# Batch 0 of a Fourier-and-mixer kernel without its feature fold: all 256 features in two products, with the carried weights and the first token layer interleaved anew

## The chip, the cores and the metric

The kernel runs on one core of one Trainium2 chip. Times are device microseconds (us) of that core, median of several executions; lower is better. Executions of one kernel differ (the six of before spread over 1.35 us or 0.22%), so a change of one microsecond needs many runs and a look at where in the execution it arises.

The engines are PE (matrix products), PEld (its weight loads), DVE, ACT and POOL (elementwise work) and SP (issues transfers). "L519" in a line of the profile is line 519 of that kernel's source. Line numbers differ between the two kernels, but tile names do not.

## The reference

```python
# x: (8, 3008, 256), w_tok1: (3008, 256), w_tok2: (256, 3008),
# w_ch1: (256, 1536), w_ch2: (1536, 256); output float32
def attn(x):
    X = np.fft.fft(x, axis=1)        # over the 3008 tokens
    X = np.fft.fft(X, axis=2)        # over the 256 features
    return X.real.astype(np.float32)

def mixer(x, w_tok1, w_tok2, w_ch1, w_ch2):
    xt = x.transpose(0, 2, 1)
    h = np.maximum(xt @ w_tok1, 0.0) @ w_tok2      # token layers
    u = x + h.transpose(0, 2, 1)
    h2 = np.maximum(u @ w_ch1, 0.0) @ w_ch2        # channel layers
    return u + h2
```

The kernel factors the long Fourier transform (3008 = 64 x 47). It adds each row of x to its mirror row (`xp` + `xm`), takes a first stage of 47 points (`pz`, copied to `z`), a second stage over the features (`pw`, copied to `w`), and a third stage (`py`, `pq`) that yields the transform. The first token layer is not applied to the transform. Its weights are carried through the third stage instead (`hp`, `hq`: the token weights `w1p`, `w1m` times the turned tables of that stage), so that it can start on `w`. Then come the second token layer (`pu`) and the channel layers, whose first product has the name `pc`.

## The kernel before

Only the opening, batch 0 ahead of its first channel product `pc`, is touched. These are its parts in the kernel before.

```python
# Turning a table: 2 x 6 transposes on PE and two wide copies on ACT,
# then a product with the mirrored identity, copied on ACT with a sign.
def turn(tab, tts, warm):
    for h in range(2):
        pt = psum.tile([P, 1024], FP16, tag="mm", name="pt", bufs=3)
        for g in range(6):
            nc.tensor.transpose(out=pt[:, g * P:(g + 1) * P],
                                in_=tab[:, 6 * h + g, :], identity=ident[:])
        copy(0, tts[0][:, 768 * h:768 * h + 768], pt[:, 0:768])
    filler(warm)                    # 128-column products that keep PE busy
# ... turn_rows(tts, sgn, warm): three products "pr", three ACT copies ...

# One group of carried weights: four products and one 512-wide copy.
def carried(tts, dst, g2, e):
    ph = ps_mm("ph")
    for k in range(2):
        g = 2 * g2 + k
        o = ph[:, k * DTOK:(k + 1) * DTOK]
        nc.tensor.matmul(o, lhsT=tts[0][:, g * P:g * P + P], rhs=w1p[:, g, :],
                         start=True, stop=False)
        nc.tensor.matmul(o, lhsT=tts[1][:, g * P:g * P + P],
                         rhs=w1m[:, NG - 1 - g, :], start=False, stop=True)
    copy(e, dst[:, 2 * g2:2 * g2 + 2, :].rearrange("p g k -> p (g k)"), ph[:])

def fold(b, engs):
    # ... for each of four slices of the tokens:
    tt(out=xp[:, t, 1:D], in0=xp[:, t, 1:D], in1=xm[0:KR, rv, D - 1:0:-1], op=add)
    # the feature fold, even and odd parts (removed for batch 0):
    tt(out=eo[:, t, 1:129], in0=xp[:, t, 1:129], in1=xp[:, t, 255:127:-1], op=add)
    tt(out=eo[:, t, 129:256], in0=xp[:, t, 1:128], in1=xp[:, t, 255:128:-1], op=sub)

def front(b):
    # ... first stage: 8 groups of products pz from eo, each copied into z ...
    for g in range(NG):                                   # NG = 12
        pw = ps_f("pw")
        nc.tensor.matmul(pw[:, 131:WD], lhsT=zb, rhs=td1[:], start=True, stop=True)
        nc.tensor.matmul(pw[:, 0:131], lhsT=za, rhs=td0[:], start=True, stop=True)
        copy(0, w[:, g, 132:WD], pw[:, 132:WD])                    # ACT
        nc.vector.scalar_tensor_tensor(                            # DVE
            out=w[:, g, 0:131], in0=alt[:], scalar=pw[:, 131:132],
            in1=pw[:, 0:131], op0=AT.mult, op1=AT.add)
        yield
    # ... batch 0: the mirror product (needs every w), tok1(0), third(0), tok1(1),
    #     each token half ending in a relu on ACT, then pu, then pc ...
```

The order in which the pieces of the opening are issued, engine by engine, is this schedule. The tables `tp` and `tq` are finished before it starts.

```python
turn(tp, tts_p, 8)
turn_rows(tts_p, 1.0, 0)
pieces = fold(0, [nc.vector] * 4)
take(pieces, 6)
table_d()
take(pieces, 6)
own = front(0)
take(own, 2)
turn(tq, tts_q, 4)
take(own, 4)
turn_rows(tts_q, -1.0, 0)
take(own, 2)
filler(8)
take(own, 2)
for g2 in range(2):
    carried(tts_p, hp, g2, g2)
for g2 in range(NG // 2):
    if g2 < 5:
        take(own, 2)
    if g2 < 4:
        carried(tts_p, hp, g2 + 2, 0)
    carried(tts_q, hq, g2, g2 < 4)
take(own, 5)
filler(12)
```

## Time and profile before

The kernel had a median of 610.72 us in three runs (609.71 to 610.97). The profiled execution took 609.52 us.

| event in the profile of before | us |
|---|---|
| first add on x (DVE) | 12.25 |
| first product `pw` | 23.29 |
| mirror product (all of `w` is copied) | 30.39 |
| products `pu` (second token layer) go on, after one at 33.59 and a wait for a relu | 35.15 |
| first product `pc` (channel layer) | 36.62 |

From the page of before: the span, busy time by engine, the granted PE clock in 40 slices of 15 us, and the last chain by engine.

```profile
span 607.7 us, 15619 instructions
PE 586.5 (97%) x6278; PEld 420.0 (69%) x6278; DVE 453.8 (75%) x1018; ACT 442.7 (73%) x996; POOL 150.1 (25%) x233
...
PEclk9999999999999999999999999999999999999999
...
PE 91%; DVE 4%; ACT 4%; issue 1%; DVEq 0%
```

PE is busy for 97% of the span and holds 91% of the chain. What the change can win lies ahead of the first `pc`, and there the chain is another one. This is the chain of before up to that point, as start, duration and what ran.

```profile
12.27 0.84 ACT tq L240
13.13 0.84 ACT tq L240
13.99 1.52 ACT tt L284 x2
...
17.79 0.96 ACT z L284 x2
18.75 1.38 ACT tt L284 x2
...
22.21 1.03 DVE z L282 x2
23.29 0.23 PE pw L460
...
25.29 0.53 DVE w L463 x2
25.82 0.60 DVE hq L282
...
34.68 0.43 ACT uu L501
35.15 0.96 PE pu L552 x3
...
36.78 1.42 PE pc L592 x6
```

The opening ran on ACT until about 20 us (sines of the tables, and the wide copies of the turned tables), then on DVE, whose `w` and `hq` lines alternate in rounds of 1.13 us. PE holds only about 2.2 us of this chain before 30 us. From the timeline of before (start, busy time, engine, line, operation, output and inputs, shapes, and in brackets how long the engine had been idle and what ended it):

```profile
12.25 0.23 DVE L411 TENSOR_TENSOR xp<-xp,xm 94x16 f16<-94x16 f16 x1
...
36.62 1.58 PE L592 MATMUL pc<-ut,wc1p 128*128 128x512 f16 x6
```

One reading needs a warning. The row PEclk shows full speed from the first slice, and a table by stretches does so too, as in this line of before (stretch in us, its length, PE busy time and instructions, granted clock, share of the transfer engines, GB/s).

```profile
17.22:20.63 3.41, 3.05 (x33) 1.00 1.40 218
```

Here the clock column says 1.00. Yet the starts of neighbouring 128-column products are 107 ns apart in that stretch, against 55 to 57 ns later. The trace has no clock record ahead of the first switch, at 20.63 us, and the column counts time without a record as full speed. So before's PE ran at half rate until 20.63 us.

### The profile page before, as it was taken

Reading aid. Unit: us, or ns where it says so; the run is one execution under the profiler, and the core shown is the slowest. Engines: PE = TensorE matmul, PEld = TensorE weight load, DVE = VectorE, ACT = ScalarE, POOL = GpSimd, SP = SyncE. Lnnn points to the kernel's source line nnn. Section 1 sums busy time; section 2 is a strip of 40 time slices with the busy share of each in tenths; the row PEclk is TensorE's granted clock in tenths of the full one; section 3 lists DMA queues with packets and bytes.
Section 4 is the critical chain, followed back from the end, with each engine's and each line's share of the span. In section 5 each row is a group of like instructions: output and inputs, shape, how many; then the busy total and the mean of one; then the engine's idle time right before and its main releaser. Section 6 shows DMA issues by size and latency. Waiting matters only on the chain.

```text
span 607.7 us, 15619 instructions
## 1 busy us (share of the span) xinstructions
PE 586.5 (97%) x6278; PEld 420.0 (69%) x6278; DVE 453.8 (75%) x1018; ACT 442.7 (73%) x996; POOL 150.1 (25%) x233
## 2 busy tenths in 40 slices
PE   1999999999999999999999999999999999999996
PEld 1756767667777677766777667766687667766675
DVE  8869689658887597757988689756979666665672
ACT  9876886777777777686777777677776877767772
POOL 8400414112242122401214222411231112111131
PEclk9999999999999999999999999999999999999999
DMA  9993924733348535663529234493242424234624
GB/s 152 210 202 90 179 57 81 134 69 70 63 92 158 69 53 86 115 108 53 91 51 176 61 75 75 77 179 53 53 74 47 92 53 81 61 70 60 90 58 100
DMA packets 86601, 56.53 MB, mean 93 GB/s; under 512 B 54864, under 2 KB 83472, under 8 KB 85776
## 3 DMA queue, kind: packets, MB, share of 16 engines
q1 hardware_dynamic: 78048, 37.84, 34.1%
q0 software_dynamic: 8256, 17.49, 16.5%
q8 instruction: 49, 0.80, 0.6%
q10 hardware_dynamic: 224, 0.20, 0.1%
q14 instruction: 24, 0.20, 0.1%
HBM read 34.98 MB, written 24.64 MB: 98 GB/s over the span
## 4 chain that ended last, share of the span: by engine, by line
PE 91%; DVE 4%; ACT 4%; issue 1%; DVEq 0%
PE pc L592 39%; PE px L633 23%; PE py L633 9%; PE pu L552 7%; PE po L690 4%; PE pt L482 3%; PE pz L433 2%; DVE w L463 1%; PE py L510 1%; PE pq L510 1%; PE pw L460 1%; PE pw L461 1%; DVE sb L609 1%; ACT tt L284 0%; DVE osb L618 0%
## 5 line engine op out<-in xcount | busy, mean ns | idle before, releaser
L595 ACT ACTIVATE c<-pc 128x512 f16<-128x512 f32 (+1 forms) x572 | 295.8, 594 | 38.8 <-PE pc L592 20.7
L618 POOL TENSOR_TENSOR osb<-osb,rt 128x256 f32<-128x256 f32 x84 | 83.0, 988 | 377.6 <-DVE osb L618 364.6
L592 PE MATMUL pc<-ut,wc1p 128*128 128x512 f16 x576 | 140.5, 379 | 0.0
L633 PEld LDWEIGHTS <-c 128*128 128x128 f16 x2016 | 121.4, 98 | 20.7 <-issue 1.3
L592 PE MATMUL pc<-ut,wc1m 128*128 128x512 f16 (+1 forms) x576 | 134.9, 370 | 0.0
L560 DVE TENSOR_TENSOR ut<-pu,yt 128x512 f16<-128x512 f32 (+1 forms) x96 | 64.7, 675 | 53.2 <-PE pu L552 53.0
L633 PEld LDWEIGHTS <-sb 128*128 128x128 f16 x1512 | 89.9, 98 | 10.7 <-DVE sb L609 0.7
L638 ACT ACTIVATE m<-px 128x256 f32<-128x256 f32 x126 | 48.5, 385 | 66.8 <-PE px L633 40.7
L592 PEld LDWEIGHTS <-wc1p 128*128 128x128 f16 x576 | 52.1, 98 | 49.2 <-issue 2.6
L592 PEld LDWEIGHTS <-wc1m 128*128 128x128 f16 x576 | 53.0, 98 | 46.4
L633 PE MATMUL px<-wst,c 128*128 128x128 f16 x1008 | 70.8, 219 | 0.2 <-DVE c L609 0.2
L633 PE MATMUL px<-wc,c 128*128 128x128 f16 x1008 | 63.1, 219 | 0.0
L609 DVE TENSOR_TENSOR sb<-c 128x768 f16<-128x768 f16 x84 | 51.2, 609 | 2.3 <-ACT c L595 2.3
L609 DVE TENSOR_TENSOR sb<-sb,c 128x768 f16<-128x768 f16 x84 | 50.3, 598 | 2.9
L284 ACT ACTIVATE z<-pz 128x480 f16<-128x480 f32 (+1 forms) x60 | 39.9, 671 | 16.9 <-PE pz L433 11.0
L618 DVE TENSOR_TENSOR osb<-py,m 128x256 f32<-128x256 f32 x84 | 35.2, 420 | 22.2 <-ACT m L638 17.4
L552 PE MATMUL pu<-w2p,uu 128*128 128x512 f16 (+1 forms) x168 | 50.0, 379 | 0.0
L463 DVE SCALAR_TENSOR_TENSOR w<-alt,pw 128x131 f16<-128x131 f16 x96 | 33.1, 351 | 21.9 <-ACT w L284 21.4
L609 DVE TENSOR_TENSOR sb<-c,sb 128x768 f16<-128x768 f16 x84 | 47.1, 561 | 0.0
L609 DVE TENSOR_TENSOR c<-c 128x768 f16<-128x768 f16 x84 | 46.6, 554 | 0.0
L517 DVE TENSOR_TENSOR yt<-py,qs 128x512 f16<-128x512 f32 x48 | 30.9, 686 | 15.1 <-ACT qs L513 15.0
L633 PE MATMUL py<-wst,sb 128*128 128x128 f16 x504 | 35.2, 219 | 0.6 <-DVE sb L609 0.6
(164 smaller groups left out, 676.3 us busy)
## 6 DMA issues: line engine op xcount, KB each, us to landing
out_dram<-osb SPq DMA_DIRECT2D x83, 256.0 KB, 3.8
xp<-in_x_dram POOLq DMA_DIRECT2D x16, 272.0 KB
out_dram<-osb SPq DMA_DIRECT2D x11, 192.0 KB, 3.1
xp<-in_x_dram POOLq DMA_DIRECT2D x16, 127.5 KB
rt<-ut SPq DMA_TRANSPOSE x96, 3.8
w2s<-in_moe_w_tok_dram POOLq DMA_DIRECT2D x1, 1504.0 KB
w1p<-in_moe_w_tok_dram POOLq DMA_DIRECT2D x2, 384.0 KB
wc<-in_moe_w_ch_dram POOLq DMA_DIRECT2D x1, 768.0 KB
```

Of the source, the lines that this page charges most:

```text
L284: nc.scalar.activation(out=out_, in_=in_, func=AFT.Copy)
L463: nc.vector.scalar_tensor_tensor(out=w[:, g, 0:131], in0=alt[:], scalar=pw[:, 131:132], in1=pw[:, 0:131], op0=AT.mult, op1=AT.add)
L517: nc.vector.tensor_tensor(out=yt[:, h, CW * c:CW * c + CW], in0=py[:], in1=qs[:], op=op)
L552: nc.tensor.matmul(pu[:, 0:n], lhsT=uu[:, th, int(minus), h, :], rhs=w2_cols(b, c)[:, th], start=(th == 0), stop=(th == 1))
L560: nc.vector.tensor_tensor(out=ut[:, h, 0:n].rearrange("p (a b) -> p a b", b=64), in0=pu[:, 0:n].rearrange("p (b a) -> p a b", b=64), in1=y ...
L592: nc.tensor.matmul(pc[:, 0:n], lhsT=wc[:, h, ct * P:(ct + 1) * P], rhs=ut[:, h, 0:n], start=(h == 0), stop=(h == 1))
L595: nc.scalar.activation(out=c1[:, ct, 0:n], in_=pc[:, 0:n], func=AFT.Relu)
L609: nc.vector.tensor_tensor(out=o, in0=x, in1=y, op=op)
L618: eng.tensor_tensor(out=o, in0=x, in1=y, op=AT.add)
L633: nc.tensor.matmul(o[:, t], lhsT=a(k)[:, f:f + P], rhs=w(k), start=(first and t == 0 and k == 0), stop=(k == HC - 1), skip_group_check=True)
L638: nc.scalar.activation(out=m[:, i], in_=pa[:, 0], func=AFT.Copy)
L690: nc.tensor.matmul(po[0:n, o:o + D], lhsT=c1[:, ct, ks * P:ks * P + n], rhs=wc2[:, ct, :], start=(ct == 0), stop=(ct == NCT - 1))
```

## The change

The intent is to shorten the opening of batch 0. The feature fold, eight DVE writes of `eo`, goes away. In its place the second stage takes all 256 features, in two accumulated products for each of the two column ranges (48 products where there were 24), with a second table `tdb`, the first one times an alternating sign. `w` is then one copy instead of an ACT copy and a DVE combine. The sines and the turning of `tq` move behind the first stage, between the `pw` products, and the carried weights `hp` and `hq` are spread over the `pw` products and the token layer. Before the first transpose, 36 products of 256 columns, whose results nobody reads, warm up PE. Later batches compute as before.

The core of the diff, with cuts marked:

```diff
+    def warm(n):
+        pw = ps_out("filler")
+        for _ in range(n):
+            nc.tensor.matmul(pw[:, 0:256], lhsT=altu[:, 0:P], rhs=altu[:, 0:256],
+                             start=True, stop=True)
 ...
-    nc.vector.scalar_tensor_tensor(out=vq[:], in0=vq[:], scalar=-float(S), in1=mq[:],
-                                   op0=AT.mult, op1=AT.add)
-    table3(tq, vq)
 ...
+    def table_b():
+        nc.vector.tensor_tensor(out=tdb[:], in0=tdu[:], in1=altu[:], op=AT.mult)
 ...
+    def fold0():
+        # ... the four adds of xp and xm, and eo for row 0 alone ...
 ...
+    def zw0():
+        # ... first stage from xp, then:
+        for g in range(NG):
+            pw = next(five)("pw")
+            for lo, hi in ((131, WD), (0, 131)):
+                for i, tab in ((0, tdu), (1, tdb)):
+                    nc.tensor.matmul(
+                        pw[:, lo:hi],
+                        lhsT=z[:, i, 2 * g:2 * g + 2, :].rearrange("p a b -> p (a b)"),
+                        rhs=tab[:, lo:hi], start=(i == 0), stop=(i == 1))
+            copy(W0_COPY[g], w[:, g, :], pw[:, 0:WD])
+            yield
 ...
-            mirrored(ps_out("pt1"))
-            uv0 = tok1(0)
-            yield
-            third(0, (0, uv0))
-            yield
-            relu(1, tok1(1))
+            third(0)
+            yield
+            pts = [ps_out("pt1") for _ in range(2)]
+            for th in range(2):
+                tok1(pts[th], th, 0)
+            yield
+            # ... then tok1(.., 1) of both halves, two sq, two uv, the relus ...
 ...
-    turn(tp, tts_p, 8)
-    turn_rows(tts_p, 1.0, 0)
-    pieces = fold(0, [nc.vector] * 4)
-    # ... the schedule printed above ...
+    warm(36)
+    turn(tp, tts_p, 0)
+    pieces = fold0()
+    take(pieces, 1)
+    table_d()
+    table_perm()
+    take(pieces, 4)
+    own = zw0()
+    nc.vector.scalar_tensor_tensor(out=vq[:], in0=vq[:], scalar=-float(S), in1=mq[:],
+                                   op0=AT.mult, op1=AT.add)
+    take(own, 3)
+    turn_rows(tts_p, 1.0, 0)
+    table_b()
+    take(own, 5)
+    table3(tq, vq)
+    take(own, 3)
+    carried(tts_p, hp, 0, 1)
+    take(own, 2)
+    carried(tts_p, hp, 1, 0)
+    take(own, 1)
+    turn(tq, tts_q, 0)
+    take(own, 2)
+    carried(tts_p, hp, 2, 1)
+    turn_rows(tts_q, -1.0, 0)
+    take(own, 2)
+    carried(tts_p, hp, 3, 1)
+    take(own, 2)
+    carried(tts_p, hp, 4, 0)
+    carried(tts_p, hp, 5, 1)
+    mirrored(state[0]["w"], ps_out("pt1"))
+    own = front(0)
+    # ... the six groups of hq, between the pieces of the token layer ...
```

## The prediction

Two passages on when PE's clock rises are cut from it where marked: they stated a rule that no trace of this case shows, and what I concluded from it. About 4 us won by the first `pw`, less about 3 given back after the mirror product, remain the net 1.0 us behind 609.6. "Its 128-column products" are those of the kernel before.

> **What bounds the kernel now.** The busy table has PE at 586.5 of 607.7 us (97%); in the chain that ended last PE holds 91%. The stretch table shows PE at 10.0 of 10 us from 40 us on: a matmul stream which the diff does not touch. Only the opening can move: the first layer product (pc) starts at 36.6 us, and until then the chain runs through ACT and DVE. Read from the timeline:
>
> - 0 to 12.3: table arithmetic on ACT; batch 0 of x has landed at about 11.7 (DMA packets).
> - 12.3 to 23.3: turning tp and tq on ACT (tt copies, 1.5 and 1.8 us each time), sine tables, and DVE folding 12.25 to 19.0 (four adds of 0.7, eight eo writes of 0.43 to 0.57). First w product at 23.3.
> - 23.3 to 30.4: six rounds of 1.13 us, set by DVE: two w combines (0.35 each) and a 512-wide cast (0.69).
> - 30.4 to 35.15: token layer; PE idles 1.14 before pu, waiting for ACT's relu.
>
> **Removed.** Eight eo writes, about 3.6 us of DVE, less about 0.6 for the edge rows; tq's sines (1.7) leave the stretch before the first w; twelve w copies that occupied both ACT (0.27) and DVE (0.35) become one copy of 259 columns on one of them (estimate 0.35 to 0.42).
>
> **Added.** 24 more pw products (about 0.056 us each, 1.3 us of PE); tdb, altu, t0h, POOL copies (off the chain). 36 warming products where PE idles.
>
> [...]its 128-column products are 107 ns apart until 19 us, 55 ns at 22.5[...]. The warming products should give 55 ns from the first transpose. That is worth little by itself: PE is not the limit there.
>
> **Moved.** Turning tq and all of hp now interleave with the w products; hq goes into the token layer. So work that leaves the first stretch is largely paid later. Laying the new order out with before's durations, each engine in order, I estimate:
>
> | event | before | after |
> |---|---|---|
> | first x add on DVE | 12.25 | 11.8 |
> | first w product | 23.3 | 19.2 |
> | mirror product (all w copied) | 30.4 | 26.4 |
> | wait before token-layer pu ends | 35.15 | 34.1 |
> | first pc | 36.6 | 35.6 |
>
> Four us are won by the first w product and kept to the mirror product. About three are given back: after it PE still carries all six hq groups (0.44 each), with ACT and DVE copies behind them, and both token halves finish together, with two sq, two uv and the relu in series before pu. Net about 1.0 us.
>
> Nothing should return this later: wc1 lands by 31.4, x of batch 1 at 43.6, against a first use at 45.6 (then 44.6).
>
> **Predicted: 609.6 us, 80% range 608.0 to 611.0.** Chances: faster by over 2% 0.01, within 2% 0.985, slower 0.005.
>
> **Right or wrong.** Right if the first pw starts near 19 us, PE shows 55 ns spacing before 14 us, the mirror product is near 26.4 and pc near 35.6, with the rest shifted whole. Wrong in the mechanism if pc moves by 4 us (carrying hq was hidden) or not at all.
>
> **What would make it wrong.** Fold adds waiting for x; w1 landing (about 19.5) holding the first carried product; PE falling back to half rate in idle gaps before 19 us (over 3 us lost); transposes queued behind the loads swallowing 1 us. Before's three runs spread 1.3 us, as much as the effect.

## The result, and the profile after

| | before | after |
|---|---|---|
| median of six runs, us | 610.58 | 611.23 |
| lowest to highest, us | 609.62 to 610.97 | 610.17 to 612.43 |
| ratio after to before | | 1.0015, 95% interval 0.9998 to 1.0032 |

Ratios are computed as the mean time of one kernel's runs over that of the other's of the same rounds, so they are not quite the ratio of the medians quoted beside them. The verdict is "same": the interval touches 1, and no difference is clear of the noise. The prediction had the class right, which was a safe forecast: 2% is 12 us, a third of the whole opening. Its time, 609.6 us, lies 1.6 us below, and its range ended at 611.0.

From the page of after, the lines that answer to those of before:

```profile
span 610.6 us, 15693 instructions
PE 594.0 (97%) x6319; PEld 425.0 (70%) x6319; DVE 453.7 (74%) x1017; ACT 441.0 (72%) x988; POOL 147.9 (24%) x232
...
PEclk9699999999999999999999999999999999999999
...
PE 92%; DVE 4%; DMA 1%; ACT 1%; issue 0%; POOL 0%; DVEq 0%; POOLq 0%
```

Two things are new: a slice of the clock row is at 6 tenths, and a transfer has entered the chain. The chain of after, up to the first `pc`:

```profile
5.27 7.93 DMA xm<-in_x_dram,ix
13.32 0.23 DVE xp L447
13.54 0.56 DVE xp L452
...
18.78 1.67 DVE z L293 x3
20.50 1.38 PE pw L519 x11
...
24.90 1.28 PE pt L261 x12
26.18 0.56 PE pw L519 x8
...
35.15 0.60 ACT hq L295
...
37.10 0.42 ACT uu L595
37.58 1.26 PE pu L664 x4
...
39.50 1.42 PE pc L704 x6
```

ACT is gone from the first 20 us: the chain now starts at the landing of x and passes through DVE, and from 20.50 us it runs on PE, which was predicted to have slack. The timeline of after shows why, on PE:

```profile
12.58 0.84 PE L261 MATMUL pt<-ident,tp 128*128 128x128 f16 x12 [1.42 <-ACT tp L245]
15.58 0.62 PE L476 MATMUL pz<-t1n,xp 94*128 94x96 f16 x10 [2.16 <-DVE xp L452]
...
20.58 0.32 PE L519 MATMUL pw<-tdu,z 128*128 128x131 f16 x1
20.69 0.32 PE L519 MATMUL pw<-tdb,z 128*128 128x131 f16 x1
...
26.46 0.22 PE L519 MATMUL pw<-tdu,z 128*128 128x131 f16 x1
26.52 0.22 PE L519 MATMUL pw<-tdb,z 128*128 128x131 f16 x1
...
30.44 0.18 PE L491 MATMUL pt<-w,perm 128*128 128x12 f16 x1
...
39.34 1.58 PE L704 MATMUL pc<-ut,wc1p 128*128 128x512 f16 x6
```

Read the rate from the distance of neighbouring starts, not from the duration of one product: here products of 0.32 us start 0.11 us apart, so they overlap. At 20.6 us two `pw` products are 110 ns apart; at 26.5 us they are 60 ns apart. The same stretch in 3.4 us pieces, cut so that the instants at which the clock switched (9.20, 16.03 and 26.27 us) fall between pieces (same columns as above; the clock ahead of 9.20 us has no record):

```profile
9.20:12.62 3.42, 2.00 (x19) 1.00 1.10 186
12.62:16.03 3.41, 1.25 (x22) 1.00 1.43 192
16.03:19.44 3.41, 3.41 (x32) 0.50 1.48 199
19.44:22.86 3.42, 2.96 (x24) 0.50 1.14 222
22.86:26.27 3.41, 3.41 (x30) 0.50 1.05 217
26.27:29.68 3.41, 3.06 (x37) 1.00 1.04 205
```

The warming products brought full rate at 9.20 us (without them, in e2 below, it came at 24.85). At 16.03 us it was taken back, and it returned only at 26.27 us, by which time almost seven of the twelve `pw` groups had been issued. The other five executions of the changed kernel have no trace, only a mean clock. It is 0.991 to 0.996 in all six, and one piece of 3.41 us at half rate takes 0.0028 off it (0.5 x 3.41 of 610 us). The end of the run, after the last product, takes off up to about 0.002 more (profiles without a half-rate piece after their first record have 0.998 to 1.000), and half rate ahead of the first record takes off nothing. From these numbers I estimate that each of them had 3 to 10 us of half rate, one to three such pieces.

Everything else in the run is the same in both kernels. Time of the profiled run less start of the first `pc` is 572.90 us for before (609.52 less 36.62) and 573.05 us for after (612.39 less 39.34), and 572.9 to 573.4 us in all fourteen profiles. So the comparison reduces to the start of the first `pc`, and to four intervals that add up to it:

| us | first x add | x add to first `pw` | `pw` to mirror | mirror to `pc` | first `pc` |
|---|---|---|---|---|---|
| before | 12.25 | 11.04 | 7.10 | 6.23 | 36.62 |
| predicted for after | 11.8 | 7.4 | 7.2 | 9.2 | 35.6 |
| after | 13.32 | 6.72 | 10.40 | 8.90 | 39.34 |

The way to the first `pw` became shorter by more than predicted, and the later give-back is near the prediction. Two terms are off: x came later, and the stretch from the first `pw` to the mirror product took 3.2 us longer than predicted.

### The profile page after: what moved, and what is told of

It reads as the page before. It is cut to its first block, busy times and chain, and to the rows that moved or that the text cites. A ratio compares the mean times of both kernels' runs of the same rounds, so it can differ in the third digit from the quotient of the medians.

```text
span 610.6 us, 15693 instructions
## 1 busy us (share of the span) xinstructions
PE 594.0 (97%) x6319; PEld 425.0 (70%) x6319; DVE 453.7 (74%) x1017; ACT 441.0 (72%) x988; POOL 147.9 (24%) x232
## 4 chain that ended last, share of the span: by engine, by line
PE 92%; DVE 4%; DMA 1%; ACT 1%; issue 0%; POOL 0%; DVEq 0%; POOLq 0%
PE pc L704 39%; PE px L745 23%; PE py L745 9%; PE pu L664 7%; PE po L802 4%; PE pt L572 4%; PE pz L476 2%; DMA xm<-in_x_dram,ix 1%; PE pq L604 1%; PE py L604 1%; PE pw L519 1%; PE pw L556 1%; DVE sb L721 1%; PE pw L555 1%; DVE w L558 1%; PE ph L400 1%
## 5 line engine op out<-in xcount | busy, mean ns | idle before, releaser
L730 POOL TENSOR_TENSOR osb<-osb,rt 128x256 f32<-128x256 f32 x84 | 80.1, 954 | 384.4 <-DVE osb L730 374.5
L721 DVE TENSOR_TENSOR sb<-c 128x768 f16<-128x768 f16 x84 | 48.1, 573 | 2.4 <-ACT c L707 2.4
L558 DVE SCALAR_TENSOR_TENSOR w<-alt,pw 128x131 f16<-128x131 f16 x84 | 29.3, 350 | 19.7 <-ACT w L295 19.1
```

What stands on the lines that cost most here:

```text
L558: nc.vector.scalar_tensor_tensor(out=w[:, g, 0:131], in0=alt[:], scalar=pw[:, 131:132], in1=pw[:, 0:131], op0=AT.mult, op1=AT.add)
L721: nc.vector.tensor_tensor(out=o, in0=x, in1=y, op=op)
L730: eng.tensor_tensor(out=o, in0=x, in1=y, op=AT.add)
```

## The experiments

My theory: the clock's return to half rate costs the `pw` stretch two to three microseconds, and the rest is the late landing of x. Rivals: (A) the twelve groups of `pw` and carried weights are limited by their copies or by something other than PE; (B) the new order of the token layer costs more than it seems; (C) the pass over `vq`, which DVE does between the adds and the copies of `z`, delays the first stage; (D) the fold itself was worth removing but its gain is hidden by ACT.

Twelve more runs were made (ten edits, and each of the two kernels once more), all correct: e1 to e4 on one chip, e5 to e8 on a second, e9 to e12 on a third, each beside its own runs of before. The summary of them first (profiled run of each; the last column is the run's median, and the ratio to before of the same rounds with its 95% interval):

| us | x add | to `pw` | to mirror | to `pc` | first `pc` | median; ratio [95%] |
|---|---|---|---|---|---|---|
| before again | 12.34 | 11.82 | 7.31 | 6.23 | 37.70 | 610.17; 0.9992 [0.9972, 1.0012] |
| after again | 12.87 | 6.42 | 9.33 | 8.89 | 37.51 | 611.05; 1.0017 [0.9996, 1.0038] |
| e1, kept warm | 13.69 | 7.89 | 8.01 | 8.89 | 38.48 | 610.69; 1.0004 [0.9991, 1.0017] |
| e2, no warming | 12.57 | 7.08 | 9.91 | 8.89 | 38.45 | 611.38; 1.0015 [1.0002, 1.0028] |
| e3, before warmed | 12.45 | 10.62 | 7.11 | 6.22 | 36.40 | 609.97; 0.9996 [0.9983, 1.0009] |
| e4, `vq` early | 13.66 | 6.70 | 10.42 | 8.90 | 39.68 | 612.09; 1.0023 [1.0011, 1.0036] |
| e5, all early, warm | 12.75 | 6.73 | 8.08 | 8.90 | 36.46 | 609.50; 0.9993 [0.9976, 1.0009] |
| e6, kept warm otherwise | 13.55 | 6.31 | 9.53 | 8.89 | 38.28 | 610.22; 0.9996 [0.9982, 1.0011] |
| e7, old order | 12.47 | 11.61 | 9.46 | 6.88 | 40.42 | 613.74; 1.0051 [1.0031, 1.0071] |
| e8, all early, cold | 13.53 | 7.54 | 6.90 | 8.89 | 36.86 | 609.43; 0.9979 [0.9964, 0.9994] |
| e9, `pw` first, warm | 13.68 | 5.84 | 6.95 | 8.98 | 35.45 | 608.70; 0.9975 [0.9959, 0.9991] |
| e10, `pw` first, cold | 12.60 | 7.53 | 6.90 | 8.98 | 36.01 | 609.83; 0.9991 [0.9976, 1.0007] |

### e1: the changed kernel, kept warm

```diff
-    warm(36)
-    turn(tp, tts_p, 0)
+    warm(44)
+    turn(tp, tts_p, 24)
 ...
-    turn_rows(tts_p, 1.0, 0)
+    turn_rows(tts_p, 1.0, 8)
     table_b()
     take(own, 5)
+    filler(16)
```

> Edit: the changed kernel with 44 instead of 36 warming products at the start, and idle-filling products after the first transposes (24), after the reversed rows of tp (8) and before the first w product (16). Theory A (PE fell back to half rate at 16 us and did the whole w stage at 110 ns a product): no half-rate piece between 12 and 27 us, w products 56 ns apart, first pc at about 36.3 us (39.3 in the changed kernel, 36.6 in the kernel before), the time about 3 us below the changed kernel, 607.5 to 609. Rival B (the new order itself is what costs: hq behind the token layer, two halves ending together): first pc stays above 38.5 us even at full rate.

Measured: full rate from 10.70 us on, with no half-rate piece. The `pw` stretch went from 10.40 to 8.01 us, with the copies and their order unchanged, so rival A does not hold for the difference. In its first piece the rate is full:

```profile
20.94:24.35 3.41, 2.75 (x39) 1.00 1.06 215
```

But the last 16 fillers shared a buffer with a copy of `z` on ACT and waited for it, so the first `pw` came about 0.8 us late. PE also waited 0.60 us for the token weights `w1m`, and x again came late (13.69 us). The first `pc` at 38.48 us misses the 36.3 us that the theory asked for, and the median of 610.69 us its 607.5 to 609. What follows: the `pw` stretch does depend on the clock, but my fillers had a price of their own, and the weights' landing appeared as a limit behind the clock.

### e2: the changed kernel without its warming products

```diff
-    warm(36)
     turn(tp, tts_p, 0)
```

> Edit: the changed kernel without the 36 warming products. Theory A says that the warmth they buy is lost at 16 us before anything that is limited by PE runs: first pc within 1 us of 39.3, the time within 1 us of the changed kernel. If the warming products are worth what they were meant for, first pc comes after 40.5 and the time is over 1 us longer.

Measured: 611.38 us, ratio 1.0015, the same as the changed kernel with them. PE reached full rate at 24.85 us. As they stand, the 36 products buy nothing. The full rate that they bring, 9.20 to 16.03 us, falls where PE waits for tables and for x.

### e3: the kernel before, warmed

```diff
-    turn(tp, tts_p, 8)
-    turn_rows(tts_p, 1.0, 0)
+    warm(66)
+    turn(tp, tts_p, 12)
+    turn_rows(tts_p, 1.0, 8)
```

(with a tile of ones and the `warm` helper added.)

> Edit: the kernel before with warming products from about 1 us on and a few more between its first products, so that PE has full rate from the first transpose. Its chain up to 20 us runs through ACT and DVE, so theory A expects little: first pc 36.0 to 36.6 (36.6 without), the time 0 to 0.7 us below the kernel before. If half rate up to 20.6 us cost the kernel before as much as it costs the changed one, it gains over 1.5 us.

Measured: full rate from 6.54 us on and not lost in the profile, and yet the first `pc` comes only 0.2 us earlier than in before (36.40 against 36.62 us), and the ratio is 0.9996. Full rate ahead of 20.6 us is worth next to nothing to the old order, whose chain runs on ACT there. Later in its opening it is worth something: three of the six executions had a mean clock of 0.997, low by about what one 3.4 us piece takes off, and took 610.44 to 610.71 us, and the three at 0.999 or 1.000 took 609.30 to 609.51. So a piece of half rate goes with about a microsecond in the old order too, wherever it fell (those executions have no trace, so this is not shown to be the cause). In the executions of before, all those with a mean clock of 0.997 or less took 610.46 us or more. But those at 0.998 or more lie anywhere from 609.45 to 612.14 us: the mean clock does not see half rate ahead of the first record.

### e4: the changed kernel with the vq pass moved ahead of the adds

```diff
     turn(tp, tts_p, 0)
+    nc.vector.scalar_tensor_tensor(out=vq[:], in0=vq[:], scalar=-float(S), in1=mq[:],
+                                   op0=AT.mult, op1=AT.add)
     pieces = fold0()
 ...
     own = zw0()
-    nc.vector.scalar_tensor_tensor(out=vq[:], in0=vq[:], scalar=-float(S), in1=mq[:],
-                                   op0=AT.mult, op1=AT.add)
     take(own, 3)
```

> Edit: the changed kernel with the vq pass of DVE (0.94 us) put back before the fold, where DVE waits 2 us for x. First w product about 0.9 us earlier (20.0 to about 19.2). Theory A: PE at half rate then runs the w stage as the limit, and starting earlier helps by at most 0.9, or not at all[...]: first pc 38.4 to 39.3, the time 0 to 0.9 us below the changed kernel.

Measured: from the x add to the first `pw` 6.70 us, against 6.72. The 0.9 us that I expected are not there. The pass is in the chain of after (16.65 us, 0.94 us), but when it is taken out, PE at half rate is next in line. The half-rate piece (10.24 us long, from 16.39 to 26.63 us) and the `pw` stretch (10.42 us) repeat those of after within 0.02 us; a second profile of after, below, has both of them shorter. The first `pc` at 39.68 us and the median of 612.09 us lie above what I expected. Rival C falls, as long as the rate is half.

### e5: everything for tq done early, and kept warm

```diff
-    warm(36)
-    turn(tp, tts_p, 0)
+    warm(44)
+    table_d()
+    # the vq pass here
+    turn(tp, tts_p, 24)
+    table3(tq, vq)
     pieces = fold0()
 ...
     take(own, 5)
-    table3(tq, vq)
+    turn(tq, tts_q, 0)
 ...            # turn_rows(tq) goes where turn(tq) was, with the old places removed
```

> Edit: the changed kernel with what waits behind x taken out of the way: vq and the argument of the sine table before the fold (DVE idles there until x lands), both sine tables before the z copies on ACT, tq turned on PE while the last z copies run, its rows reversed earlier; 44 warming products and 24 filling ones. Theory A (clock, landing of x and what stands in the line behind it): full rate from 10 us, first w product about 6.5 us after the first x add, mirror product 7 us after that, first pc 35.0 to 36.0 if x lands at 13 us or earlier; time 608.3 to 609.8, below the kernel before. Rival B (the new token-layer order is the cost): first pc above 37.5.

Measured: full rate from 10.10 us on; first `pc` at 36.46 us, 2.9 us earlier than in the profile of after; median 609.50 us. It misses the upper end of what I expected, 36 us, by half a microsecond. (Two of the six executions had a mean clock of 0.997 and took 610.88 and 610.91 us; the four at 1.000 took 609.28 to 609.60.) This is the wait of PE in it that explains the rest (engine, product and what it waited for; us in total, times, longest us):

```profile
PE ph L400 <- DMA w1m<-in_moe_w_tok_dram: 1.5, 1, 1.5
```

With the clock restored, the carried products are early enough to wait for their weights. The last packet of these weights lands at 21.07 us in this run, and between 20.0 and 22.5 us in all of them (20.04 us in before, 20.72 in after).

### e6: the changed kernel kept warm with fillers from another pool

```diff
     turn_rows(tts_p, 1.0, 0)
     table_b()
-    take(own, 5)
+    take(own, 3)
+    filler_mm(16)
+    take(own, 2)
+    filler_mm(8)
```

(with the first two edits of e1; `filler_mm` is `filler` on the buffers of the carried products.)

> Edit: the changed kernel with the clock kept at full rate like e1_keep_warm, but the later filling products moved to another PSUM tag and ahead of the last z products, since in e1_keep_warm they waited for a z copy and held the first w product by about 0.8 us. Theory A: no half-rate piece, first w product at most 7.2 us after the first x add, first pc 36.5 to 37.8, the time 609.0 to 610.2. If keeping the clock is worth nothing, first pc stays at 38.4 or later, as in e1_keep_warm and e2_no_start_warm.

Measured: the fillers no longer wait, and the first `pw` comes 6.31 us after the x add, the shortest way of any kernel in this order. But the weights landed late in this run, at 22.30 us, and PE waited 1.3 us for them, so the `pw` stretch is 9.53 us at full rate. 38.28 us for the first `pc` lies outside the 36.5 to 37.8 us that I had given. The clock alone does not make the `pw` stretch short. The landing of the weights is a second limit that the half rate had hidden.

### e7: no fold, but the old order

The schedule is that of the kernel before, with `fold0()` for `fold(0, ..)`, `zw0()` for the first two stages, the `vq` pass and the sines of `tq` early as before, and no warming.

```diff
-    warm(36)
-    turn(tp, tts_p, 0)
+    # the vq pass
+    turn(tp, tts_p, 8)
+    table3(tq, vq)
+    turn_rows(tts_p, 1.0, 0)
     pieces = fold0()
 ...
+    for g2 in range(NG // 2):
+        if g2 < 5:
+            take(own, 2)
+        if g2 < 4:
+            carried(tts_p, hp, g2 + 2, 0)
+        carried(tts_q, hq, g2, g2 < 4)
     mirrored(state[0]["w"], ps_out("pt1"))
     own = front(0)
+    take(own, 5)
```

> Edit: one part of the change alone: no feature fold for batch 0 (two products per group, as in the changed kernel), but the kernel before's order of work: tq turned before the first w product, hp and hq carried between the w products, no warming products, token layer afterwards. Theory A: first w product 20 to 21, w stage limited by PE at about 8 us if PE has full rate by then (24 more products than the kernel before) and up to 3 us more if not; first pc 35.5 to 37.5; the time 608.8 to 610.8. Rival B (carrying hq inside the token layer is the cost) expects it over 1.5 us below the changed kernel at the same clock, so first pc at or below 36.5.

Measured: 613.74 us, ratio 1.0051: slower than before, where I had expected 608.8 to 610.8 us. The first `pw` came at 24.08 us (expected 20 to 21), 11.61 us after the x add, against 11.04 in before, and the first `pc` at 40.42 us. Taking the feature fold away gained nothing there, since ACT's turning of the tables sets that time (rival D holds for the old order). The `pw` stretch, now with 48 products and partly at half rate (23.66 to 27.08 us), became 2.4 us longer. The fold's removal pays only through the new order.

### e8: e5 without warming

```diff
-    warm(44)
     table_d()
 ...
-    turn(tp, tts_p, 24)
+    turn(tp, tts_p, 0)
```

> Edit: e5_all_early without its 44 warming and 24 filling products. Theory A: [...]the w stage runs at 110 ns a product for part of its time: first pc 1 to 2.5 us later than e5_all_early. If the clock does not matter, the two agree within 0.5 us.

Measured: first `pc` at 36.86 us against 36.46 in e5, medians 609.43 and 609.50 us. Without warming, PE reached full rate only at 22.18 us, and that cost nothing, less than I had expected: x came 0.78 us later in this profile than in e5, and from the x add to the first `pc` e8 took 23.33 us, e5 23.71. At half rate the first products come 0.8 us later, but no time is then lost waiting for the weights, which landed at 20.89 us. As long as the weights were the limit, the clock was free. (The interval of e8's ratio is clear of 1 too: this order beats before by 0.2%.) If e8 had been the only test of the clock, it would have spoken against my theory.

### e9: all twelve groups of pw ahead of the carried weights, warm

```diff
     turn(tq, tts_q, 0)
-    take(own, 3)
-    carried(tts_p, hp, 0, 1)
-    take(own, 2)
-    carried(tts_p, hp, 1, 0)
-    take(own, 1)
-    turn_rows(tts_q, -1.0, 0)
-    # ... four more groups of hp, between pairs of pw ...
+    take(own, 12)
+    turn_rows(tts_q, -1.0, 0)
+    for g2, e in enumerate((1, 0, 1, 1, 0, 1)):
+        carried(tts_p, hp, g2, e)
```

(against e5.)

> Edit: e5_all_early with all twelve w groups ahead of the first carried product; in e5_all_early PE stood 1.55 us in line for the last part of w1 to land with nine w groups behind it. Theory C (the floor is the landing of w1, 21.5 to 23 us in the profiles, and the w products are the work that does not need it): PE does not wait for w1 or under 0.4 us, mirror product earlier than 26.5, first pc 34.3 to 35.3 (36.46 in e5_all_early), time 607.6 to 608.8. If the floor lies in the copies of ACT and DVE instead, first pc stays within 0.5 us of 36.4.

Measured: no wait for the weights is left. The longest waits of PE between 11 and 37 us are these two:

```profile
PE pz L476 <- DVE xp L452: 0.9, 1, 0.9
PE pu L664 <- ACT uu L595: 0.8, 1, 0.8
```

The first `pc` comes at 35.45 us although x was late (13.68 us), the earliest of all the profiles. I had expected 35.3 us at most, so this is a narrow miss. The median is 608.70 us, ratio 0.9975 with an interval clear of 1: this kernel beats the kernel before, if only by a quarter of a per cent. It beats the changed kernel as well: e12, the changed kernel again, ran on the same chip, and all six executions of e9 (608.62 to 610.20 us) are below all four of that (610.65 to 612.52 us). The slowest execution of e9 is the one with a low mean clock, 0.996; the other five, at 0.998 or more, lie between 608.62 and 608.81 us. Its token layer is that of the change and takes 8.98 us from mirror to `pc`. Rival B falls, as far as it claims more than was predicted. In this order the rest of the run is some 0.4 us longer (573.36 us, and 573.44 in e10). It arises at once: ACT starts its first copy of `c` 1.22 us after the first `pc` in e9 and e10, against 0.81 in after, and the seventeenth `pc` comes 0.30 us later. What holds ACT there is not shown.

### e10: e9 without warming

```diff
-    warm(44)
     table_d()
 ...
-    turn(tp, tts_p, 24)
+    turn(tp, tts_p, 0)
```

(against e9.)

> Edit: e9_w_first without the warming and filling products. In e8_all_early_cold the half rate lasted to 22.2 us and cost nothing, because PE would have stood waiting for w1 until 21.5 anyway. Theory A and C together: here the w products fill that wait, so half rate costs again: first pc 1 to 2.5 us later than e9_w_first, 35.5 to 37.5. If the clock costs nothing, within 0.5 us of e9_w_first.

Measured: from the x add to the first `pw` 7.53 us, against 5.84 in e9; `pw` stretch the same, since full rate came at 20.24 us, just as it began. Ahead of that PE was the limit: in e10 it was busy without a break (its clock has no record yet, but the twelve transposes in this stretch start 107 ns apart), in e9 it was not.

```profile
16.83:20.24 3.41, 3.41 (x38) 1.00 1.47 211
16.25:19.66 3.41, 2.84 (x42) 1.00 1.50 205
```

The first line is e10's, the second e9's. Median 609.83 against 608.70 us. With the wait for the weights out of the way, the clock is worth 1.1 us in the medians and 1.7 us in that interval. Unlike e8, this pair shows the clock by itself.

### e11 and e12: both kernels once more

No edit. They were run to see how much of the two profiles is repeatable.

> The kernel before, unchanged, for a second profile: x lands between 12 and 13.7 us as in the others, and since its chain to 20 us runs through ACT, first pc is 36.6 to 37.7 whatever the landing; a later first pc with the clock restored after 20.6 would show its spread of 609.5 to 611 to be the clock's.

> The changed kernel, unchanged, for a second profile. Theory A: again a half-rate piece of 6.8 to 10.2 us that covers part of the w stage, first pc 37.5 to 39.7, later the longer the half-rate piece overlaps the w stage and the later x lands; x lands between 12.2 and 13.7.

Measured: before again has its first `pc` at 37.70 us (610.61 us in that run) where its first profile had 36.62. Its clock became full at 24.63 us, 4.0 us later. So the profile from which I predicted was that of a fast execution of before. The time of the run differs by 1.09 us and the first `pc` by 1.08, so in this one pair the distance between the two clusters of before arises ahead of the first `pc`, as the clock would have it. After again has it at 37.51 us: x came at 12.87 us, and the half-rate piece was 6.8 us long, not 10.2.

```profile
12.71:16.12 3.41, 1.70 (x27) 1.00 1.43 191
16.12:19.54 3.42, 3.13 (x27) 0.50 1.47 198
19.54:22.95 3.41, 2.95 (x25) 0.50 1.14 229
22.95:26.36 3.41, 3.08 (x38) 1.00 1.03 213
```

In the same order of work on PE there are now four profiles (and e1, with its fillers) which differ in how much of the `pw` stretch lies in half rate:

| | half rate within the `pw` stretch, us | `pw` stretch, us |
|---|---|---|
| after | 6.23 | 10.40 |
| e4 | 6.27 | 10.42 |
| e2 | 5.20 | 9.91 |
| after again | 3.66 | 9.33 |
| e1 (kept warm, with fillers) | 0 | 8.01 |

From the ends, (10.40 - 9.33) / (6.23 - 3.66) = 0.42 us are lost per microsecond of half rate. Carried on to none, this gives about 7.8 us, an estimate, and e1 measured 8.01. By the same estimate the half rate cost about 2.6 us in the first profile of after and 1.5 us in the second.

## Why the prediction was right and where it was wrong

Against the prediction, with the mean of the two profiles of each kernel:

| us | first x add | to `pw` | to mirror | to `pc` | first `pc` |
|---|---|---|---|---|---|
| before, mean of two | 12.30 | 11.43 | 7.21 | 6.23 | 37.16 |
| predicted for after | 11.8 | 7.4 | 7.2 | 9.2 | 35.6 |
| after, mean of two | 13.10 | 6.57 | 9.87 | 8.90 | 38.43 |
| measured less predicted | +1.3 | -0.8 | +2.7 | -0.3 | +2.8 |

- **The bound and the place.** Right. PE bounds the run from the first `pc` on, the diff leaves that part alone, and 573 us follow it in both kernels. The class was right for this reason.
- **The way to the first w product.** The step was right and its gain is larger than predicted: 4.9 us shorter than in before, where the two predicted intervals differ by 3.6. The fold and ACT's tables both left it; e7 shows that the fold alone, in the old order, gains nothing. How the gain divides between the two in the new order was not measured.
- **The give-back after the mirror product.** Right: predicted 9.2 us, measured 8.90, against 6.23 in before. Carrying `hq` there and finishing both token halves together costs 2.7 us, as the prediction's "about three".
- **The failed step.** "The warming products should give 55 ns from the first transpose. That is worth little by itself: PE is not the limit there." They gave it from 9.20 to 16.03 us, and it was then taken back. The sentence judged PE by before's order, in which it was no limit that early (in e3 full rate from 6.54 us on brought the first `pc` forward by 0.2 us). In the new order PE is the limit between the first `pw` and the mirror product, with twice the products and the carried weights between them, and it went through 6.2 us of the 10.4 (first profile) and 3.7 of the 9.3 (second) at 107 to 110 ns per product. The row "mirror product 26.4" rests on that sentence: 7.2 us for the stretch, measured 10.40 and 9.33. The prediction named the risk (PE falling back in idle gaps, over 3 us lost), and bet against it. It came to pass in both profiles, and by the estimate from the mean clocks in every execution.
- **Where PE fell back.** In the piece 12.62 to 16.03 us of after PE was busy for 1.25 of 3.41 us, and it stood still for 2.16 us before the first `pz`, waiting for x. Half rate then lasted 10.24 us. In the other profiles that lost the rate, PE had been busy in the 3.41 us ahead of the loss for 0.93 us (e4, then 10.24 us of half rate), 1.59 us (e7, then 3.42) and 1.70 us (after again, then 6.83). In e6 PE was busy for 1.80 of the 3.41 us from 20.42 us, in e5 for 1.86 of those from 20.34, and full rate went on. In after PE was then busy for all of 16.03 to 19.44 us and stayed at half rate until 26.27. In e7 the rate rose after 3.42 us, of which PE was busy for 3.35. What makes the clock fall, and what sets how long it stays there, is not shown: no run changes that alone. (Transposes run faster at full rate too: the twelve at 12.58 us took 0.84 us, twelve in before at half rate 1.46.)
- **The first x add.** Off by 1.3 us, the second mis-sized term. I had read the landing of x from a run of packets that ended at 11.7 us. The last packet in that profile lands at 11.80, and the first add starts at 12.25; in after they are at 12.87 and 13.32, so 0.45 us pass between the two in both. On top of this the landing varies from run to run in two clusters, with the first add at 12.25 to 12.87 us in eight profiles and at 13.32 to 13.69 in six. The changed kernel itself showed both, and e8, without warming, was late too, so neither the change nor the warming alone explains it. The traces narrow it down: POOL issues the transfers of x at the same times in all fourteen, within 0.04 us, but the last 8704-byte packet of `xp` ends at 9.14 to 9.51 us in the six late profiles (9.14 in after) and at 7.69 to 8.17 in the others (7.98 in before). So the delay is there before the gather of the mirror rows (`xm`) ends, in the first transfers of the run. What makes it late stays open. Before might absorb a late x, because its chain runs on ACT at that time (no profile of it had one); after cannot, since its chain starts there.
- **The carried weights' landing.** The prediction had it as a risk ("w1 landing (about 19.5)"). In after the half rate hid it. With the clock restored it held PE for 0.6 us (e1), 1.3 us (e6) and 1.5 us (e5), and e9 shows that it can be avoided by order alone.
- **The base.** The events were counted from before's profile, one of its faster executions. By that profile the predicted `pc` at 35.6 us would have meant 608.5 us (609.52 less 1.0). The 609.6 us fits the median of 610.72 less the 1.0 us (the prediction does not say from which it was counted). What was measured follows from the terms above: a first `pc` at 38.4 us, plus 573 us, is 611.4, and the median was 611.23.

What is shown: the half-rate piece in both profiles of after, its absence in e1, e5, e6 and e9, and a `pw` stretch that follows it wherever PE does not wait for the weights. e9 against e10 shows its price where no other limit hides it. In the change's own order restoring the clock is worth little in the medians, since the weights then hold PE: 610.69 (e1) and 610.22 us (e6), against 611.23 and 611.05 for after, on different chips. What is not shown: whether the wait for x in front of `pz` (2.16 us in the first profile of after) made the clock fall back.

## What to carry to other kernels

Before calling PE "not the limit" in a stretch, ask whether it will be the limit in the new order. If so, count the time at the rate that PE will really have there, from the spacing of neighbouring starts. Warm-up work is worth what it gives to the products which are next in line: put it close ahead of them (in after a wait of 2.16 us stood between, and the rate was lost; in e9 the longest wait there was 0.9 us, and it was kept), and check in the trace that the rate was still there when they came. When one limit is lifted and the time does not follow, look at once for the one that it hid, here the landing of the weights; a pair of kernels that differ in the first limit alone tells little until the second is out of the way (e5 and e8 against e9 and e10).
